# Attention in front of two feed-forward layers: transposes by row halves, a new order in a step, and another way for the softmax's inverse

## Chip, cores and metric

The kernel runs on one core of a Trainium2 chip. The metric is the device time of one execution in microseconds; lower is better. TensorE is PE in the profile (its weight loads PEld), VectorE is DVE, ScalarE is ACT, GpSimd is POOL and SyncE, which issues nearly all DMAs here, is SP.

## What is computed

```python
scores = scale * (q @ k.T)                    # B 2, H 8, S 576, D 64
x = psi_rel / psi_i                           # log1p of |i-j| over log1p of max(i,1)
bias = relu(x * w1 + b1) @ w2                 # 32 hidden units, one value per head
attn = exp(s - max(s)); attn /= sum(attn) + 1e-9     # s = scores + bias
x = (attn @ v) as (1152, 512)
x = prelu(x @ w_in, alpha) @ w_out            # 512 -> 2048 -> 512
out = (P(h) / Q(h)) @ w_out2, h = x @ w_in2   # rational activation
```

All inputs and the output are fp32.

## The kernel before

The attention is cut into nine blocks of 128 query rows (`BLOCKS`, four row blocks of each batch and one that holds the last 64 rows of both), and each block into four steps of two heads: 36 steps, numbered 0 to 35. `scores` (L313) makes a step's two 128x576 score planes in four banks of PSUM, the two heads on the two halves of the array's rows. `row_max` (L333, DVE) adds the bias, writes the sum to SBUF and keeps the row's extreme in `nm`. `expo` (L345, ACT) takes the exponential and its row sum. `flip` (L353) transposes the step's 128x1152 plane on PE, nine blocks of 128x128: four of each head into a bank of `ps_t` (two buffers of one bank), and the ninth, which spans both heads, into a spare place beside the next step's scores. `flip_out` copies the blocks to SBUF: two copies of 128x512 on ACT (in a few steps, by the table `ON`, one of them on DVE) and one of 128x128 on DVE. `values` (L379) multiplies them with V two steps after the scores. So in the place of step n, PE runs the scores of n, the transposes of n-1 and the values of n-2.

The bias is made beside that. Each of 36 `row`s takes four `hidden` operations (L222, 128x576, on DVE or ACT), eight matmuls in two halves (`bias_mm`, L235), an eviction for each half (`bias_out`, L249, DVE or ACT) and a DMA into the bias tile (`bias_move`, L267, on SP's queue). The eight rows of the first tile come before step 0, the other 28 within steps up to step 27.

When a block's fourth step is done, `inverse` (L398, DVE) makes the eight inverse row sums of each query. Blocks 0 to 5 turn them by a matmul with the identity (`inverse_flip`, L405), copy that out, store it to DRAM and read it back spread over partitions (`inverse_spread`, L412); blocks 6 to 8 spread it by eight matmuls (`inverse_on_tensor`, L429). `block_out`, `block_scale` and `block_split` (L421 to L451) take the block from PSUM, multiply it and split it into a high and a low part for the next layer; the low part is GpSimd's only work in the attention.

The order of all this is a list of due times (class `Agenda`): every piece is put on it with a time worked out from the tables' numbers (`Z`), the list is sorted, and each engine gets its instructions in that order. The numbers set an order, not a duration. From step 28 on, the bias is done and the first five weight units of the feed-forward layers (`unit_one`, `unit_two`, L654 on) come between the steps, on ACT and DVE. After step 35 the two feed-forward layers take PE to the end.

```python
ag.at(next_t + Z[f"new_flip{u}"] if new else t + DT + Z["flip0"] + Z["flip1"] * u, flip, n, u)
ag.at(t + DT + Z["fout0"] + Z["fout1"] * u, flip_out, n, u)
```

## Time and profile before

| what | us |
|---|---|
| three timed runs | 600.17, 601.75, 601.97 |
| median | 601.75 |
| span of the profiled execution, first to last instruction | 600.0 |
| time around the span, by the three runs | 0.2 to 2.0 |
| PE busy in the span | 584.8 (97%) |
| DVE, ACT, POOL busy | 496.7, 433.1, 23.7 |
| scores of step 0, 3, 28, 35 start at | 20.90, 37.79, 153.77, 184.99 |

The profiled execution's own time is not listed apart from its span; the table's fourth line says what can lie around it. A busy time is a union of spans, so an engine with overlapping instructions is not counted twice. A row of a timeline merges neighbours of one kind and gives their start, the time from the first start to the last end, and their count. A fp32 matmul leaves two records, a transpose one. Starts that follow each other give the time that a piece takes on PE, since ends overlap the next piece.

### The profile page before, as it was taken

The page shows a single profiled execution, that of the slowest core. Times are in us where ns is not written, and L with a number is a line of the kernel's source. Part 1 is how long each engine was busy: PE and PEld are TensorE (multiplying, and loading weights), DVE is VectorE, ACT ScalarE, POOL GpSimd, SP SyncE. Part 2 cuts the span into 40 slices and gives each one's busy share as a digit, 9 for nine tenths or more (in the row PEclk, how much of TensorE's full clock was granted, in tenths as well). Part 3 has the DMA queues.
Part 4 walks back from the last instruction along what each step waited for, and adds up shares of the span by engine and source line. Part 5 has one row for each costly group of instructions (what it writes and reads, how often), then busy time and mean ns, then how long its engine had stood idle before and what let it go on. Part 6 is the DMA issues. An engine that isn't in the chain of part 4 may idle for free.

```text
span 600.0 us, 11975 instructions
## 1 busy us (share of the span) xinstructions
PE 584.8 (97%) x4798; PEld 504.4 (84%) x4798; DVE 496.7 (83%) x837; ACT 433.1 (72%) x728; POOL 23.7 (4%) x23
## 2 busy tenths in 40 slices
PE   8899999999988999999999999999999999999997
PEld 4366666676757999999999999998999999899985
DVE  6688787877798767689998779989999999779784
ACT  6678989889777666676675567787777887655660
POOL 0000000000000000000000302000000000000000
PEclk9899999999999999999999999999999999999999
DMA  5894333342632334445555376867000000001011
GB/s 167 256 239 117 86 85 91 88 118 64 165 103 76 108 104 141 138 143 148 173 162 162 129 210 215 230 200 262 9 1 1 0 1 1 2 1 52 1 52 52
DMA packets 41238, 65.31 MB, mean 109 GB/s; under 512 B 4016, under 2 KB 23776, under 8 KB 41184
## 3 DMA queue, kind: packets, MB, share of 16 engines
q1 hardware_dynamic: 41040, 64.21, 36.5%
q8 instruction: 37, 0.61, 0.4%
q10 hardware_dynamic: 144, 0.35, 0.2%
q14 instruction: 17, 0.14, 0.1%
HBM read 47.35 MB, written 6.58 MB: 90 GB/s over the span
## 4 chain that ended last, share of the span: by engine, by line
PE 84%; DVE 8%; ACT 3%; DMA 2%; issue 2%; SPq 0%; DVEq 0%; ACTq 0%
PE ops L695 30%; PE hps L680 30%; PE bps L244 7%; PE s L326 6%; PE pv L389 5%; PE tp L365 4%; DVE p L338 1%; DVE mid L623 1%; PE s L361 1%; DVE w L649 1%; DMA away<-mid 1%; DVE mid L626 1%; DMA bias<-be 1%; DMA sm<-in_small_dram 1%; ACT p L349 1%
## 5 line engine op out<-in xcount | busy, mean ns | idle before, releaser
L680 PE MATMUL hps<-xh,w 128*128 128x384 f32 x768 | 204.1, 336 | 0.5 <-DVE nm L338 0.5
L680 PEld LDWEIGHTS hps<-xh,w 128*128 128x128 f32 x768 | 139.6, 188 | 1.9 <-DVE nm L338 0.7
L680 PE MATMUL hps<-xl,w 128*128 128x384 f32 x384 | 128.7, 335 | 0.0
L695 PE MATMUL ops<-g,w 128*128 128x384 f32 x576 | 104.5, 336 | 0.0
L695 PE MATMUL ops<-w,g 128*128 128x512 f32 x432 | 102.5, 392 | 1.2 <-DVE acc L767 1.2
L695 PEld LDWEIGHTS ops<-g,w 128*128 128x128 f32 x576 | 100.8, 188 | 0.0
L695 PEld LDWEIGHTS ops<-w,g 128*128 128x128 f32 x432 | 80.7, 188 | 17.6 <-issue 1.5
L349 ACT ACTIVATE p<-p,nm 128x576 f32<-128x576 f32 x72 | 55.6, 773 | 24.2 <-DVE nm L338 24.0
L680 PEld LDWEIGHTS hps<-xl,w 128*128 128x128 f32 x384 | 72.1, 188 | 0.9
L750 ACT CAST g<-n 128x768 fp32r<-128x768 f32 x48 | 40.0, 834 | 38.3 <-DVE n L714 26.5
L338 DVE CUSTOM_DVE_ANT_0 p<-s,bias 128x576 f32<-128x576 f32 x72 | 52.2, 755 | 17.6 <-PE s L326 8.7
L623 DVE SCALAR_TENSOR_TENSOR mid<-mid,raw 128x512 int32<-128x512 int32 x64 | 47.8, 747 | 13.5 <-ACT mid L615 13.3
L244 PE MATMUL bps<-h,w2s 128*32 128x288 f32 x576 | 51.2, 420 | 4.1 <-DVE be L258 2.5
L230 DVE TENSOR_SCALAR h<-tt,sc,nb 128x576 f32<-128x576 f32 x98 | 52.3, 573 | 0.0
L755 DVE TENSOR_TENSOR g<-n,g 128x768 fp32r<-128x768 f32 x48 | 46.5, 969 | 6.6 <-ACT g L750 6.6
L626 DVE SCALAR_TENSOR_TENSOR mid<-raw,mid 128x512 int32<-128x512 int32 x64 | 47.4, 740 | 2.2
L389 PEld LDWEIGHTS pv<-pt,v 128*32 128x32 f32 (+1 forms) x1320 | 40.8, 116 | 7.7 <-issue 1.8
L645 ACT CAST w<-mid 128x512 fp32r<-128x512 f32 x64 | 39.2, 614 | 10.8 <-PE hps L680 10.6
L389 PE MATMUL pv<-pt,v 128*32 128x128 f32 (+2 forms) x1320 | 46.6, 267 | 0.0
L619 ACT ACTIVATE raw<-raw 128x512 int32<-128x512 uint32 x64 | 43.4, 678 | 4.3 <-DMA raw<-in_moe_w_out_dram 2.6
L326 PE MATMUL s<-kt,q 64*128 64x288 f32 (+1 forms) x320 | 45.9, 433 | 0.0
L649 DVE TENSOR_TENSOR w<-mid,w 128x512 fp32r<-128x512 f32 x64 | 44.6, 699 | 0.0
(73 smaller groups left out, 723.4 us busy)
## 6 DMA issues: line engine op xcount, KB each, us to landing
raw<-in_moe_w_in_dram SPq DMA_DIRECT2D x32, 512.0 KB, 4.5
raw<-in_moe_w_out_dram SPq DMA_DIRECT2D x32, 512.0 KB, 3.7
bias<-be SPq DMA_DIRECT2D x32, 288.0 KB, 3.9
away<-mid SPq DMA_DIRECT2D x16, 256.0 KB, 4.8
mid<-away SPq DMA_DIRECT2D x16, 256.0 KB, 4.7
v<-in_vp_dram SPq DMA_DIRECT2D x10, 256.0 KB, 5.3
kt<-in_kT_dram SPq DMA_DIRECT2D x8, 288.0 KB, 5.8
out_dram<-acc SPq DMA_DIRECT2D x9, 256.0 KB, 2.1
```

What stands on the lines that cost most here:

```text
L230: nc.vector.tensor_scalar(out=h, in0=x, scalar1=sc[:, k : k + 1], scalar2=nb1, op0=ALU.mult, op1=ALU.max)
L244: nc.tensor.matmul(out=ps[32 * c : 32 * c + 32], lhsT=w2s, rhs=hid[j, r, c][:, u * HALF : (u + 1) * HALF], start=True, stop=True,)
L326: nc.tensor.matmul(out=pps[n, u][cols, w, :HALF], lhsT=queries[k][rows, hp, cols], rhs=KT[bb][rows, hp, w * HALF : (w + 1) * HALF], start= ...
L338: nc.vector.tensor_tensor_reduce(out=ptile[n][:, u, :].rearrange("p (w j) -> p w j", w=2), in0=pps.pop((n, u))[:, :, :HALF], in1=bias[j][: ...
L349: nc.scalar.activation(out=p, in_=p, func=AF.Exp, bias=nms.pop((n, u)), scale=-1.0, accum_out=sums[k][:, h : h + 1])
L389: nc.tensor.matmul(out=pv[64 * u + d : 64 * u + d + wide, hp, cols], lhsT=V[bb][:, j, 2 * hp + u, d : d + wide], rhs=pt[:, 4 * u + j if j ...
L623: nc.vector.scalar_tensor_tensor(out=m, in0=m, scalar=3, in1=raw[:, :, 0], op0=ALU.logical_shift_left, op1=ALU.bitwise_or)
L626: nc.vector.scalar_tensor_tensor(out=m, in0=raw[:, :, 1], scalar=-(2 ** 31), in1=m, op0=ALU.bitwise_and, op1=ALU.bitwise_or)
L649: nc.vector.tensor_tensor(out=w[:, 1, :], in0=mids.pop(j), in1=w[:, 0, :].bitcast(F32), op=ALU.subtract)
L680: nc.tensor.matmul(out=ps, lhsT=a, rhs=b, start=(i == 0), stop=(i == len(prs) - 1))
L695: nc.tensor.matmul(out=ops[ly, c, m], lhsT=a, rhs=b, start=(f == fs[0] and i == 0), stop=(f == fs[-1] and i == 2))
L755: nc.vector.tensor_tensor(out=gt[:, 1], in0=tmp.pop(p), in1=gt[:, 0].bitcast(F32), op=ALU.subtract)
```

## The change

`flip` now takes each block of 128x128 as two halves of 64 rows: each is a transpose of 64x128 with a 64x64 identity, and the two halves go to two banks and use the two halves of the array's rows, as the scores do. `ps_t` becomes one buffer of two banks, and the scores' tile one buffer of four banks (`s4`), in which the ninth block's halves lie. `flip_out` copies all eight blocks with one ACT instruction of 128x1024 (in steps 32 and 34 one half each on ACT and DVE). The order is written from labels of a step: the ninth block first, then the eight, one bias row for each of the steps 1 to 26, and from step 27 on other labels. Two rows of the second bias tile (`at_once`) move ahead of step 0. The inverse of blocks 0 to 7 is turned by one DVE transpose in 32x32 blocks, stored as 128 rows of 128 bytes (`inverse_store`) and read back spread; only block 8 is spread by matmuls. GpSimd's branches (`split_pool`, `again_pool`) are not in `ON`, so those copies stay where they were. The tables of numbers are new throughout; two lines of `ON` stand for them here.

```diff
@@ ON, Z (tables)
-    "first_hidden_scalar_2", "first_hidden_scalar_6", "flip_vector_28", "flip_vector_32",
+    "first_bias_scalar_6", "first_bias_scalar_7", "first_bias_scalar_8", "first_hidden_scalar_2",
...
@@ pools and first constants
-    ps_t = open_pool("ps_t", 2, "left", PSUM)
+    ps_t = open_pool("ps_t", 1, "left", PSUM)
     ps_b = open_pool("ps_b", 1, "left", PSUM)
-    ps_s = open_pool("ps_s", 2, "right", PSUM)
+    open_pool("ps_f", 2, "right", PSUM)
+
+    def scores_psum():
+        close_pool("ps_f")
+        open_pool("ps_s", 1, "right", PSUM)
...
+    inv = ac.tile([P, 2, 32], F32, name="inv")
+    nc.vector.memset(inv[:, 0], 0.0)
...
@@ bias rows
+    def at_once(j, r):
+        return j == 0 or j == 1 and r < 2
+
     def bias_mm(j, r, u):
-        if j > 0:
+        if not at_once(j, r):
             ps = ps_b.tile([P, HALF], F32, tag="b", name="bps")
             bps[j, r, u] = ps
         else:
             if u == 0:
-                bps[j, r] = ps_s.tile([P, 2, 512], F32, tag="s", name="bps2")
+                pool = pools["ps_f" if j == 0 else "ps_t"][1]
+                bps[j, r] = pool.tile([P, 2, 512], F32, tag="f" if j == 0 else "t", name="bps2")
             ps = bps[j, r][:, u, :HALF]
...
@@ scores
+        s4 = pools["ps_s"][1].tile([P, 2, 2, 512], F32, tag="s", name="s")
         for u in range(2):
-            pps[n, u] = ps_s.tile([P, 2, 512], F32, tag="s", name="s")
+            pps[n, u] = s4[:, u]
...
-        spare[n] = pps[n, 1][:, 1, HALF : HALF + P]
+        spare[n] = s4[:, :, 1, HALF : HALF + 64]
...
@@ flip, flip_out
-    def flip(n, u):
-        p = ptile[n]
-        if u == 0:
+    def flip(n, cols):
+
+        p = ptile[n].rearrange("p u j -> p (u j)")
+        if cols == 8:
             ptt[n] = pt_p.tile([P, 9, P], F32, tag="pt", name="pt")
-
-        beside = u == 2 and FIRST <= n + 1 < LAST
-        tp = spare[n + 1] if beside else ps_t.tile([P, 512], F32, tag="t", name="tp")
-        if u == 2:
-            nc.tensor.transpose(out=tp[:, :P], in_=p.rearrange("p u j -> p (u j)")[:, 512:640], identity=ident)
-        else:
-            for j in range(4):
-                o = 64 * u + j * P
-                nc.tensor.transpose(out=tp[:, j * P : (j + 1) * P], in_=p[:, u, o : o + P], identity=ident)
-        tps[n, u] = tp
-
-    def flip_out(n, u):
-        tp, pt = tps.pop((n, u)), ptt[n]
-        if u == 2:
-            nc.vector.tensor_copy(out=pt[:, 8, :], in_=tp[:, :P])
-        else:
-            out = pt[:, 4 * u : 4 * u + 4, :].rearrange("p j i -> p (j i)")
-            if u == 1 and f"flip_vector_{n}" in ON:
-                nc.vector.tensor_copy(out=out, in_=tp)
-            else:
-                nc.scalar.copy(out=out, in_=tp)
+            if n + 1 == NSTEP:
+                tps[n, 8] = ps_b.tile([P, HALF], F32, tag="b", name="tp8")[:, :P]
+                nc.tensor.transpose(out=tps[n, 8], in_=p[:, 512 : 512 + P], identity=ident)
+                return
+            out, blocks = spare[n + 1], [(0, 512)]
+        else:
+            out = ps_t.tile([P, 2, 512], F32, tag="t", name="tp")
+            blocks = [(64 * j, j * P if j < 4 else j * P + P) for j in range(8)]
+        tps[n, cols] = out
+        for o, a in blocks:
+            for w in range(2):
+                half = slice(64 * w, 64 * w + 64)
+                nc.tensor.transpose(out=out[:, w, o : o + 64], in_=p[half, a : a + P], identity=ident[half, half])
+
+    def flip_out(n, cols):
+        tp, pt = tps.pop((n, cols)), ptt[n]
+        if cols == 8:
+            out = pt[:, 8] if n + 1 == NSTEP else pt[:, 8].rearrange("p (w i) -> p w i", w=2)
+            nc.vector.tensor_copy(out=out, in_=tp)
+            return
+        out = pt[:, :8].rearrange("p j (w i) -> p w j i", w=2)
+        tp = tp.rearrange("p w (j i) -> p w j i", i=64)
+        if f"flip_vector_{n}" in ON:
+            nc.scalar.copy(out=out[:, 0], in_=tp[:, 0])
+            nc.vector.tensor_copy(out=out[:, 1], in_=tp[:, 1])
+        else:
+            nc.scalar.copy(out=out, in_=tp)
...
-        wide = 32 if FIRST <= n + 2 < 28 else D
+        wide = 32 if n + 2 < 27 else D
...
@@ inverse
     def inverse(k):
-        rs = sm_p.tile([P, H], F32, tag="rs", name="rs")
-        nc.vector.tensor_scalar_add(rs, sums.pop(k), 1e-9)
-        nc.vector.reciprocal(out=rs, in_=rs)
-        nc.vector.tensor_scalar_mul(rs, rs, WUP ** -3)
+        rs = inv[:, 0, :H].rearrange("p (u c) -> p c u", u=2)
+        nc.vector.tensor_scalar_add(rs, sums.pop(k).rearrange("p (c u) -> p c u", u=2), 1e-9)
+        nc.vector.reciprocal(out=inv[:, 0, :H], in_=inv[:, 0, :H])
+        nc.vector.tensor_scalar_mul(inv[:, 0, :H], inv[:, 0, :H], WUP ** -3)
         rts[k] = rs
-
-    def inverse_flip(k):
-        tp = ps_t.tile([P, 512], F32, tag="t", name="tp")
-        nc.tensor.transpose(out=tp[:H, :P], in_=rts[k], identity=ident)
-        rt = xu_p.tile([H, P], F32, tag="rt", name="rt")
-        nc.vector.tensor_copy(out=rt, in_=tp[:H, :P])
-        rts[k] = rt
+        if not by_tensor(k):
+            nc.vector.transpose(out=inv[:, 1], in_=inv[:, 0])
+
+    def inverse_store(k):
+        rd = dr_p.tile([4, 32, 32], F32, tag="rd", name="rd")
+        nc.sync.dma_start(out=rd.rearrange("q f i -> (q f) i"), in_=inv[:, 1])
+        rts[k] = rd
 
     def inverse_spread(k):
-        rd = dr_p.tile([H, P], F32, tag="rd", name="rd")
-        nc.sync.dma_start(out=rd, in_=rts.pop(k))
-        rb = xu_p.tile([P, 4, P], F32, tag="rb", name="rb")
+        rb, rd = xu_p.tile([P, 4, 4, 32], F32, tag="rb", name="rb"), rts.pop(k)
         for u in range(2):
-            src = rd.rearrange("(c u) i -> u c i", u=2)[u : u + 1]
-            nc.sync.dma_start(out=rb[64 * u : 64 * u + 64], in_=src.to_broadcast([64, 4, P]))
-        xus[k] = rb
+            src = rd[:, 4 * u : 4 * u + 4].rearrange("q c i -> q (c i)").unsqueeze(0)
+            nc.sync.dma_start(
+                out=rb[64 * u : 64 * u + 64].rearrange("p q c i -> p q (c i)"), in_=src.to_broadcast([64, 4, P])
+            )
+        xus[k] = rb.rearrange("p q c i -> p c q i")
...
     def by_tensor(k):
-        return k >= 6
+        return k == 8
...
@@ block_split
-        nc.scalar.copy(out=xh, in_=xu)
+        if k < 8 and "split_pool" in ON:
+            nc.gpsimd.tensor_copy(out=xh, in_=xu)
+        else:
+            nc.scalar.copy(out=xh, in_=xu)
...
@@ the agenda
     def step_time(n):
+        return T0 + DT * min(n, NB_) + DTL * max(n - NB_, 0)
+
+    for r in range(8):
+        at0 = Z["row0"] + (r - 1) * Z["row_step"]
+        bias_rows(0, r, Z["row0"] + r * Z["row_step"], Z["row_step"], at0, Z["row_step"])
+    ag.at(T0 - 0.05, scores_psum)
+    STEP_OF = {(j, r): 8 * j - 9 + r for j in range(1, 5) for r in range(n_rows(j))}
+    for (j, r), n in STEP_OF.items():
+        if at_once(j, r):
+            t = T0 + Z["pre"] + Z["pre_step"] * r
+            if r == 0:
+                ag.at(0.1, bias_tile, j)
+            for c in range(4):
+                ag.at(t + Z[f"pre_hid{c}"], hidden, j, r, c)
+            for u in range(2):
+                ag.at(t + Z["pre_mm"] + 0.1 * u, bias_mm, j, r, u)
+                ag.at(t + Z["pre_out"] + 0.1 * u, bias_out, j, r, u)
+            ag.at(t + Z["pre_out"] + 0.3, bias_move, j, r)
...
@@ a step
+        ag.at(label("flip", n + 1), flip, n, 8)
+        ag.at(label("flip", n + 1) + 0.05, flip, n, 0)
+        ag.at(label("fout8", n + 1), flip_out, n, 8)
+        ag.at(label("fout", n + 1), flip_out, n, 0)
+        ag.at(label("values", n + 2), values, n)
...
```

A step on PE, before, in steps 3 to 26 (`s` scores, `tp` and the first `s<-ident,p` transposes, `bps` bias, `pv` values; the last row comes in every fourth step):

```order
L326 MATMUL s<-kt_132,q 128x288 x4
L361 MATMUL s<-ident,p 128x128
L365 MATMUL tp<-ident,p 128x128 x8
L244 MATMUL bps<-h,w2s 32x288 x4
L389 MATMUL pv<-pt,v_133 32x128 x20
L244 MATMUL bps<-h,w2s 32x288 x4
L407 MATMUL tp<-ident,rs 8x128
```

and with the change:

```order
L325 MATMUL s<-kt_134,q 128x288 x4
L369 MATMUL s<-ident,p 128x64 x2
L369 MATMUL tp<-ident,p 128x64 x16
L261 MATMUL bps<-h,w2s 32x288 x4
L395 MATMUL pv<-pt,v_135 32x128 x20
L261 MATMUL bps<-h,w2s 32x288 x4
```

The places of the pieces are the same; nine transposes became eighteen of half the width, and the transpose of the inverse is gone from PE.

ACT in a step, before (`p` exponentials, `pt` the copy of the transposes, `h` a hidden row, `be` a bias eviction, `xu` a block's copy):

```order
L349 ACTIVATE p,sums<-p,nm 128x576
L228 ACTIVATE h<-tt,sm,sc 128x576
L377 COPY pt<-tp 128x512
L423 COPY xu<-pv 128x512
L349 ACTIVATE p,sums<-p,nm 128x576
L377 COPY pt<-tp 128x512
L256 ACTIVATE be<-bps,cv 128x288
```

and with the change:

```order
L383 COPY pt<-tp 128x2x8x64
L348 ACTIVATE p,sums<-p,nm 128x576 x2
L273 ACTIVATE be<-bps,cv 128x288
L461 CAST xh_892<-xu 128x4x128
L241 ACTIVATE h<-tt,sm,sc 128x576
```

One copy of four dimensions takes the place of two, it stands ahead of both exponentials of the step, and the eviction and the hidden rows follow them.

PE at the first steps, before, from the half bias row ahead of step 0's scores (`wps` are matmuls that only keep PE busy):

```order
L244 MATMUL bps<-h,w2s 32x288 x4
L326 MATMUL s<-kt_131,q 128x288 x4
L186 MATMUL wps<-ident 128x128 x2
L244 MATMUL bps<-h,w2s 32x288 x8
L326 MATMUL s<-kt_131,q 128x288 x4
L244 MATMUL bps<-h,w2s 32x288 x4
L365 MATMUL tp<-ident,p 128x128 x4
L244 MATMUL bps<-h,w2s 32x288 x4
L365 MATMUL tp<-ident,p 128x128 x4
L361 MATMUL tp<-ident,p 128x128
```

and with the change, from the first of the two bias rows that moved ahead:

```order
L261 MATMUL bps_332<-h,w2s 32x288 x8
L199 MATMUL wps<-ident 128x128 x2
L261 MATMUL bps_360<-h,w2s 32x288 x8
L325 MATMUL s<-kt_133,q 128x288 x4
L199 MATMUL wps<-ident 128x128 x2
L325 MATMUL s<-kt_133,q 128x288 x4
L369 MATMUL s<-ident,p 128x64 x2
L369 MATMUL tp<-ident,p 128x64 x16
L261 MATMUL bps<-h,w2s 32x288 x8
L325 MATMUL s<-kt_133,q 128x288 x4
```

The bias rows that stood between the scores of steps 0 and 1 now stand ahead of step 0, and step 1's scores follow step 0's at once.

## Rows read from the trace of the kernel before

**Rows 1.** Busy time by stretch: window, length, busy us per engine (instructions), granted clock, DMA.
```profile
0.00:37.79 37.79, 32.44 (x318) 17.53 (x318) 26.23 (x61) 25.47 (x42) 0.70 (x6) 0.95 0.80 224
37.79:153.77 115.98, 115.76 (x1819) 77.71 (x1815) 92.39 (x246) 101.34 (x216) 6.41 (x5) 1.00 0.38 100
153.77:184.99 31.22, 27.36 (x340) 20.62 (x336) 24.61 (x58) 26.16 (x57) 2.56 (x2) 1.00 0.48 137
...
200.00:300.00 100.00, 100.00 (x585) 99.58 (x585) 79.50 (x123) 66.94 (x114) 1.29 (x1) 1.00 0.46 138
```

**Rows 2.** Timeline of PE, one step: start, us, engine, line, operation, tiles, shape, count.
```profile
51.74 1.24 PE L326 MATMUL s<-kt,q 64*128 64x288 f32 x8
52.91 0.33 PE L361 MATMUL s<-ident,p 128*128 128x128 f32 x1
53.08 1.04 PE L365 MATMUL tp<-ident,p 128*128 128x128 f32 x8
54.05 0.69 PE L244 MATMUL bps<-h,w2s 128*32 128x288 f32 x8
...
56.34 0.51 PE L326 MATMUL s<-kt,q 64*128 64x288 f32 x2
```

**Rows 3.** Timeline of PE's weight loads in the same step, the transposes.
```profile
52.91 0.14 PEld L361 LDWEIGHTS s<-ident,p 128*128 128x128 f32 x1 [0.38 <-ACT p L349]
52.97 0.91 PEld L365 LDWEIGHTS tp<-ident,p 128*128 128x128 f32 x8
```

**Rows 4.** Weight loads of that step's scores, two short windows.
```profile
51.74 0.19 PEld L326 LDWEIGHTS s<-kt,q 64*128 64x128 f32 x2 [0.47 <-DVE h L230]
...
51.85 0.19 PEld L326 LDWEIGHTS s<-kt,q 64*128 64x128 f32 x2
```

**Rows 5.** That step's last two pairs of scores on PE, two short windows.
```profile
52.33 0.41 PE L326 MATMUL s<-kt,q 64*128 64x288 f32 x2
...
52.58 0.41 PE L326 MATMUL s<-kt,q 64*128 64x288 f32 x2
```

**Rows 6.** Timeline of PE after step 35: the values matmuls of the last block.
```profile
190.08 1.39 PE L389 MATMUL pv<-pt,v 128*64 128x64 f32 x40
```

**Rows 7.** Timeline of ACT in a step: a copy of transposes and what follows it.
```profile
87.57 0.57 ACT L377 COPY pt<-tp 128x512 f32<-128x512 f32 x1
88.04 0.50 ACT L256 ACTIVATE be<-bps,cv 128x288 f32<-128x288 f32 x1
```

**Rows 8.** The page's groups: copies on ACT.
```profile
L750 ACT CAST g<-n 128x768 fp32r<-128x768 f32 x48 | 40.0, 834 | 38.3 <-DVE n L714 26.5
...
L645 ACT CAST w<-mid 128x512 fp32r<-128x512 f32 x64 | 39.2, 614 | 10.8 <-PE hps L680 10.6
```

**Rows 9.** Timeline of DVE: the first and the last operation of an inverse.
```profile
82.74 0.16 DVE L400 TENSOR_SCALAR rs<-sums 128x8 f32<-128x8 f32 x1
...
83.18 0.17 DVE L402 TENSOR_SCALAR rs<-rs 128x8 f32<-128x8 f32 x1
```

**Rows 10.** Timeline of PE, the first steps.
```profile
25.94 1.19 PE L244 MATMUL bps<-h,w2s 128*32 128x288 f32 x8 [2.54 <-DVE be L258]
27.06 2.17 PE L326 MATMUL s<-kt,q 64*128 64x288 f32 x8
...
37.79 1.24 PE L326 MATMUL s<-kt,q 64*128 64x288 f32 x8
```

**Rows 11.** Timeline of DVE: the second row maximum of step 0.
```profile
24.70 0.75 DVE L338 CUSTOM_DVE_ANT_0 p<-s,bias 128x576 f32<-128x576 f32 x1
```

**Rows 12.** Busy time by stretch, columns as in the first group.
```profile
26.00:28.00 2.00, 2.00 (x12) 0.95 (x14) 0.86 (x2) 1.98 (x5) 0.00 (x0) 0.50 1.04 363
```

**Rows 13.** Timeline of PE: an inverse on PE and two steps of the tail.
```profile
164.45 1.09 PE L434 MATMUL tp<-ident,rs 128*64 128x128 f32 x16
...
176.45 0.33 PE L361 MATMUL s<-ident,p 128*128 128x128 f32 x1 [2.21 <-ACT p L349]
...
181.67 0.33 PE L361 MATMUL s<-ident,p 128*128 128x128 f32 x1 [1.64 <-ACT p L349]
```

More of the change, by code (lines that the diff above doesn't have):

```diff
@@ L252, in bias_out @@
         out, add = bev[j, r], cv[:, int(on_scalar(j, r, 2)) : int(on_scalar(j, r, 2)) + 1]
-        if j > 0:
+        if not at_once(j, r):
             half, ps = out[:, u * HALF : (u + 1) * HALF], bps.pop((j, r, u))
@@ L276, in bias_again @@
     def bias_again(h):
-        nc.vector.tensor_copy(out=bias[4][64:, h : h + 2], in_=bias[4][:64, h : h + 2])
-    def bias_rows_beside(j, r, at, step, at0, step0):
-        z, z0 = step / 4.1, step0 / 4.1
-        for c in range(4):
-            ag.at(at0 + z0 * Z[f"hidden{c}"], hidden, j, r, c)
-        for u in range(2):
-            x = at + Z[f"bias_mm{u}"] * z
-            n = max((n for n in range(FIRST, LAST) if step_time(n) <= x), default=None)
-            if n is None:
-                ag.at(x, bias_mm, j, r, u)
-                t = at + Z[f"bias_out{u}"] * z
-            else:
-                t = max(x, step_time(n) + Z["beside"])
-                ag.at(t, bias_mm, j, r, u)
-                key = "scalar" if f"bias_scalar_{j}{u}" in ON else "vector"
-                t = max(step_time(n) + Z[f"bo_{key}{int(t - step_time(n) >= Z['values'])}"], t + 0.1)
-            ag.at(t, bias_out, j, r, u)
-        ag.at(max(at + Z["bias_move"] * z, t + 0.1), bias_move, j, r)
+        eng = nc.gpsimd if "again_pool" in ON else nc.vector
+        eng.tensor_copy(out=bias[4][64:, h : h + 2], in_=bias[4][:64, h : h + 2])
     def bias_rows(j, r, at, step, at0, step0):
@@ L434, in inverse_on_tensor @@
             nc.tensor.matmul(
[L435 removed]
+                out=tp[64 * u : 64 * u + 64, c], lhsT=rts[k][:, c, u : u + 1].to_broadcast([P, 64]), rhs=ident,
                 start=True, stop=True,
@@ L441, in block_scale @@
         xu, rb = xus[k]
+        if not by_tensor(k):
+            xu = xu.rearrange("p c (q i) -> p c q i", q=4)
         nc.vector.tensor_tensor(out=xu, in0=xu, in1=rb, op=ALU.mult)
@@ L470, in step_time, with label @@
     def step_time(n):
[L471 to L487 removed]
+        return T0 + DT * min(n, NB_) + DTL * max(n - NB_, 0)
[15 more added lines that the diff above has]
+            ag.at(t + Z["pre_out"] + 0.3, bias_move, j, r)
+            continue
+        t = step_time(n)
+        h = t - DT
+        if r == 0:
+            ag.at(t + Z["bias_o1"] + 0.15, bias_tile, j)
+        for c in range(4):
+            ag.at(h + Z[f"hid{c}"], hidden, j, r, c)
+        for u in range(2):
+            ag.at(t + Z[f"bias_b{u}"], bias_mm, j, r, u)
+            ag.at(t + Z[f"bias_o{u}"], bias_out, j, r, u)
+        ag.at(t + Z["bias_o1"] + 0.2, bias_move, j, r)
+    EARLY = step_time(STEP_OF[4, 3]) + Z["bias_o1"] + 0.3
+    def label(key, n):
+        return step_time(n) + Z[key + ("_tail" if n >= NB_ else "")]
     for n in range(NSTEP):
```

91 lines of the change are left out of this document (35 added, 56 removed), and 24 rows, old and new, of the table Z.

## Prediction

> **What bounds the kernel now.** I read three views in this order: busy time by stretch, the timeline of each engine in one step, and the weight loads beside it.
>
> The stretches [rows 1] cut the span at the scores of steps 3, 28 and 35. From step 3 to 28, 115.98 us, PE is busy 115.76, ACT 101.34 and DVE 92.39: PE bounds the 25 steps, at 4.64 us each, and ACT is next at 4.05. From step 28 to 35, 31.22 us, PE has 27.36 and ACT 26.16: neither fills it. From 200 us on PE is full (100.00 of 100), so what attention saves before that arrives at the end whole, and what ACT or DVE save there arrives not at all.
>
> One step on PE [rows 2], by starts: the scores 1.17, the first transpose 0.17, the other eight 0.97, the rest 2.29, together 4.60. Eight transposes take 1.04 with 0.27 for the last one, so each follows the one before after 0.11. Its stream has 128 columns.
>
> The weight loads of the transposes [rows 3] say what else stands in those 0.11: the second load starts 0.06 after the first, when PE comes from other work and no stream holds it back; only then do eight loads take 0.91, one in 0.11. So the load of 128 columns of a transpose needs no more than 0.06, and the stream sets the 0.11. In the scores [rows 4] two loads of 64 rows start together (count 2, 0.19 in all), and the next two 0.11 later: the halves of the rows load side by side, but a load of an ordinary fp32 matmul is slower than that of a transpose.
>
> **The change, part by part.**
>
> *Row halves on PE.* Nine transposes become nine pairs. A pair streams 64 columns. The nearest stream of that width is in the values of the last block [rows 6]: 40 records on two halves of the columns, 20 pairs in 1.39, under 0.07 a pair, and 0.06 if the last one's end is some 0.2 as elsewhere. The load needs 0.06 too if it stays as it is at full height. I take 0.06, since both rows that bear on it say so. The ends are 0.05 (half of 0.11) and 0.22 (two halves one behind the other). At 0.06 the step loses 9 x 0.05 = 0.45.
>
> *No change of the array's division between scores and transposes.* Before, the last two pairs of scores start at 52.33 and 52.58 [rows 5], 0.25 apart, yet the first transpose follows only after 0.33, and the second follows the first after 0.17 instead of 0.11 [rows 2]: together about 0.15 a step, which should go, as the halves use the rows as the scores do. No row shows the two behind each other, so the bounds are 0 and 0.15; I take 0.15. PE's step is then 4.60 - 0.45 - 0.15 = 4.0.
>
> *The copies on ACT.* Two of 512 columns become one of 1024. Now one takes 0.47 from start to start [rows 7], two 0.94. From 512 to 768 columns a cast grows from 614 to 834 ns [rows 8], 0.86 ns a column, so 512 more columns add 0.44: about 0.91. ACT gains 0.03 a step, nothing that counts; if the copy's four dimensions cost extra, up to 0.2. The split between ACT and DVE stays about even, and no work goes to GpSimd. ACT's 4.05 a step is therefore the new bound, just above PE's 4.0.
>
> *The inverse.* PE loses a transpose of 8 columns in six of the 25 steps, no dearer than the first of a step (0.33, [rows 2]), and in the tail one of the two spreads by matmuls of 1.09 [rows 13] before step 35 for block 6 and one for block 7. DVE loses a small copy and gains a transpose of 128x32: between 0.17, an operation on 128x8, and 0.75, a row maximum [rows 9, 11]; I take 0.2, as it is nearer to the first. The inverse now stands ahead of the next step's row maxima, so in every fourth step these wait for the last exponential and for four operations, 0.6 for three of them [rows 9] and 0.2: that delays ACT's exponentials by 0 to 0.8, and I expect the copy, which now precedes them on ACT, to cover it. The store of 128 short rows and the two reads have more than a step before the scaling needs them; for blocks 6 and 7 they are six DMAs more on SP's queue. Behind each store a bias move waits, which has two steps of slack: nothing.
>
> *Steps 3 to 28.* PE needs 24 x 4.0 + 3 = 99, ACT 101, DVE 92. Engines so close cannot all be full; I add 4 for waits on each other and take 105.5. Gain 10.5 (5 to 14).
>
> *The front.* The first row maxima wait for the bias and end at 25.45 [rows 11]. Before, PE stood still 2.54 until 25.94, made a half bias row first and started step 1's scores at 27.06 [rows 10], which took 2.17 as the granted clock was 0.50 there, the 1.2 GHz level [rows 12]. Step 3 starts 10.7 after that [rows 10], with five half rows and an idle stretch in between. With the two rows moved ahead, step 1 can start near 25.5, step 2 when DVE has made three hidden rows, two maxima, one eviction and one copy, some 3.7 later, and step 3 one step after that: 33.5 against 37.79. The halved clock may still meet it, and the moved rows may hold step 0 back. I take 3.5 (0 to 5).
>
> *The tail.* PE stood still 2.21 and 1.64 for exponentials [rows 13]. Its 27.36 shrink by 7 x 0.6 and two spreads to about 21; ACT's 26.16 hardly change. So ACT sets it: 26.5 for 31.22, gain 4.7 (1 to 6). Step 35 on: the same pieces, nothing.
>
> **Sum.** 10.5 + 3.5 + 4.7 = 18.7. The profiled span of 600.0 becomes 581.3. The median of the runs, 601.75, lies 1.75 above that span; I carry the same distance, 583.0.
>
> **A rule against it.** The rows on which the 0.06 rests are those of the transposes at full height; the scores' rows show 0.11 for 128 columns at half height. If a half transpose loads as a score does, a pair takes 0.11, and halving the stream wins nothing; that is the first rival below. The Trainium skill, "TensorE: Matmul & The Clock Gate", section "LDWEIGHTS (loading the stationary operand)", has it so: a load's time goes by its columns at 1.2 GHz and not by its rows, by which 128 columns are estimated at 107 ns. The trace agrees in the scores (0.11) and not in the transposes (0.06).
>
> **The rivals.**
>
> 1. *A pair takes 0.11.* For it: the loads of the scores [rows 4], the only ones at half height. Against it: the 0.06 between the first two loads of a transpose [rows 3]. PE's step is 4.45, 24 x 4.45 + 3.4 = 110.2, with 0.9 for waits 111, gain 5; the tail, on ACT, keeps 4.4, the front 3.2: 601.75 - 12.6 = 589.
>
> 2. *The steps stay at 4.6, held by ACT.* One copy for both heads, one buffer of two banks, and the exponentials behind the copy: flips, copy, exponentials and next flips form one ring. For it: ACT already waits for DVE and PE in each step, and 4.05 of work leaves little room. Against it: the copy and the exponentials take about 2.5, and the remaining 1.5 of ACT's work lies where PE makes the next transposes. Then 24 x 4.6 + 3.5 = 114, gain 2, with 5.5 of front and tail: 594, to 598 if the tail stays too.
>
> 3. *Slower: the halves go one behind the other.* If transposes of 64 rows don't run side by side, a pair takes 0.22, PE's step 4.45 + 9 x 0.11 = 5.4, and the 25 steps 24 x 5.4 + 4.4 = 134, 18 more than now; the tail gains nothing, the front 2. 601.75 + 18 - 2 = 618. It decides from about 0.155 a pair, where the steady steps lose what front and tail give. Against it: the scores do run so [rows 4]. For it: no row shows a transpose on part of the rows.
>
> **How the numbers follow.** Runs of this kernel lie 0.3% apart, so a change under 0.3% can't be told from none. Forecast 0.60, first rival 0.17, second 0.11, third 0.09; 0.03 for mishaps that eat the gain. The forecast alone runs from 576 (front 5, waits of 1) to 588. In it lies the case that the 0.15 between scores and transposes stays: PE's step 4.15, 24 x 4.15 + 3 = 103 with the same 4 for waits, 585. The range 575 to 597 takes in the first two rivals and leaves out the third. Faster 0.88, same 0.03, slower 0.09.
>
> **What would show it.** In the profile after: the eighteen transposes of a step within about 0.6 and the weight loads in pairs 0.06 apart (0.11: rival 1; each half alone: rival 3); no gap between scores and transposes; scores of neighbouring steps about 4.2 apart, ACT busy over 95% between steps 3 and 28 (PE waiting for `p` with ACT full is the forecast, PE waiting with ACT idle is rival 2); step 3 near 34, step 28 near 140, step 35 near 166; PE full from 200 us on as before. A start of step 3 later than 37, or idle PE in the feed-forward layers, would make the prediction wrong in a way that I have not priced.

## The result, and the profile after

The changed kernel takes 575.1 us (median; 573.6 to 576.9), the kernel before in the same session 601.9: a ratio of 0.956, with an interval of 0.9538 to 0.9582. The forecast was 583.0, the range 575 to 597. The sign is right, but the gain is 26.8 where 18.7 was forecast, the median lies in the range by 0.1 us, two of the four runs (573.6, 574.7) lie below it, and the band of 576 to 588 that the prediction gave to its own mechanism is missed. The profiled execution is the fastest of the four runs; its span is 571.9 us, 28.1 less than that of before. By the stretches of the prediction, in spans:

| stretch | before | after | gain | forecast |
|---|---|---|---|---|
| to step 3's scores | 37.79 | 33.54 | 4.25 | 3.5 |
| step 3 to 28 | 115.98 | 99.89 | 16.1 | 10.5 |
| step 28 to 35 | 31.22 | 26.20 | 5.0 | 4.7 |
| step 35 to the end | 415.0 | 412.3 | 2.75 | 0 |

Busy time by stretch, after (columns as in [rows 1]):

```profile
0.00:33.54 33.54, 28.90 (x336) 16.63 (x336) 24.66 (x60) 26.61 (x41) 0.70 (x6) 1.00 0.77 224
33.54:133.43 99.89, 99.34 (x2018) 72.75 (x2015) 90.48 (x247) 97.74 (x190) 7.85 (x6) 1.00 0.51 127
133.43:159.63 26.20, 22.90 (x367) 17.39 (x367) 22.67 (x58) 24.34 (x49) 1.27 (x1) 1.00 0.55 156
```

In the 25 steps PE and ACT are now both full to within 0.6 and 2.2 us. In the tail ACT is the fullest, as forecast.

One step on PE and its weight loads, after:

```profile
94.17 1.24 PE L325 MATMUL s<-kt,q 64*128 64x288 f32 x8
95.24 0.22 PE L369 MATMUL s<-ident,p 64*128 64x64 f32 x2
95.30 0.67 PE L369 MATMUL tp<-ident,p 64*128 64x64 f32 x16
95.89 0.69 PE L261 MATMUL bps<-h,w2s 128*32 128x288 f32 x8
...
98.16 1.24 PE L325 MATMUL s<-kt,q 64*128 64x288 f32 x8
```

```profile
95.00 0.14 PEld L369 LDWEIGHTS s<-ident,p 64*128 64x128 f32 x2
95.24 0.58 PEld L369 LDWEIGHTS tp<-ident,p 64*128 64x128 f32 x16
```

The first pair starts 1.07 after the scores (1.17 before, [rows 2]) and the next 0.06 later (0.17 before). Sixteen loads take 0.58 with 0.14 for the last: eight pairs, 0.06 apart. The first two loads start while the last scores still stream. From the scores to the bias row it is 1.72, where it was 2.31.

ACT in the steps, after, from copy to copy:

```profile
79.99 1.02 ACT L383 COPY pt<-tp 128x1024 f32<-128x1024 f32 x1
...
92.13 1.01 ACT L383 COPY pt<-tp 128x1024 f32<-128x1024 f32 x1
93.04 0.78 ACT L348 ACTIVATE p<-p,nm 128x576 f32<-128x576 f32 x1
...
96.19 1.01 ACT L383 COPY pt<-tp 128x1024 f32<-128x1024 f32 x1
```

The copy takes 0.91 to the next start, and four steps take 16.20, 4.05 each, with no gap on ACT; the next four take 16.09. The groups of ACT in these 25 steps (shape and count, busy us, mean ns, idle before them):

```profile
L348 ACT ACTIVATE p<-p,nm 128x576 f32<-128x576 f32 x50 | 38.7, 784 | 0.6 <-DVE nm L337 0.6
L383 ACT COPY pt<-tp 128x1024 f32<-128x1024 f32 x24 | 24.3, 1014 | 1.1 <-PE tp L369 1.0
```

Before, the same group of exponentials had 14.6 us of idle time in front of it, for row maxima.

Steps of PE range from 3.92 to 4.41, apart from step 6 (4.62, a wait for V) and step 27 (3.08, without a bias row). The 4.41 stands once, in step 15; on PE and on DVE it is:

```profile
81.90 1.24 PE L325 MATMUL s<-kt,q 64*128 64x288 f32 x8
...
85.68 0.69 PE L261 MATMUL bps<-h,w2s 128*32 128x288 f32 x8
86.31 1.24 PE L325 MATMUL s<-kt,q 64*128 64x288 f32 x8
```

```profile
82.17 0.69 DVE L450 TENSOR_TENSOR xu<-xu,rb 128x512 f32<-128x512 f32 x1 [0.27 <-issue]
82.78 1.07 DVE L243 TENSOR_SCALAR h<-tt,sc,nb 128x576 f32<-128x576 f32 x2
83.76 0.75 DVE L337 CUSTOM_DVE_ANT_0 p<-s,bias 128x576 f32<-128x576 f32 x1
...
85.12 0.51 DVE L275 TENSOR_SCALAR be<-bps,cv 128x288 f32<-128x288 f32 x1
```

In one step of four VectorE multiplies a block by its inverse. The row maximum then starts 1.86 after the scores (1.33 to 1.45 in the steps beside it), the eviction ends at 85.63, and the second half bias row, which needs the one buffer that it empties, starts at 85.68: PE waits some 0.45, which the modelled ends of the values hide in its busy time. In the same step of the next blocks (11, 19, 23) the step takes 4.05 or 4.06. Of all steps of 3.99 and more, but for steps 4, 6 and 20, the second half bias row starts 0.05 or 0.06 after VectorE's eviction ends; in the steps of 3.92 to 3.94 it follows by 0.09 to 0.13. By the starts, the 25 steps cost PE 97.2 of its own work (24 x 3.92 + 3.08) and 2.7 beyond it, 0.7 of them in step 6.

### The profile page after: what moved, and what is told of

Read it like the earlier page. It is cut to its first block, busy times and chain, and to the rows that moved or that the text cites. A ratio compares the mean times of both kernels' runs of the same rounds, so it can differ in the third digit from the quotient of the medians.

```text
span 571.9 us, 12499 instructions
## 1 busy us (share of the span) xinstructions
PE 559.1 (98%) x5063; PEld 494.8 (87%) x5063; DVE 489.0 (86%) x835; ACT 432.5 (76%) x697; POOL 23.5 (4%) x23
## 4 chain that ended last, share of the span: by engine, by line
PE 88%; DVE 4%; DMA 3%; ACT 3%; issue 1%; SPq 0%; ACTq 0%
PE hps L703 35%; PE ops L718 35%; PE bps L261 6%; PE pv L395 5%; PE s L325 5%; DMA v<-in_vp_dram 2%; PE tp L369 2%; DVE p L337 1%; ACT h L241 1%; DMA rd<-inv 1%; ACT p L348 1%; DMA sm<-in_small_dram 1%; ACT be L280 0%; DVE mid L646 0%; DVE mid L649 0%
## 5 line engine op out<-in xcount | busy, mean ns | idle before, releaser
L773 ACT CAST g<-n 128x768 fp32r<-128x768 f32 x48 | 40.0, 834 | 28.1 <-DVE n L737 19.6
L646 DVE SCALAR_TENSOR_TENSOR mid<-mid,raw 128x512 int32<-128x512 int32 x64 | 46.4, 726 | 8.0 <-ACT mid L638 7.8
L243 DVE TENSOR_SCALAR h<-tt,sc,nb 128x576 f32<-128x576 f32 x98 | 51.0, 573 | 0.5 <-PE bps L261 0.4
L395 PE MATMUL pv<-pt,v 128*32 128x128 f32 (+2 forms) x1300 | 47.8, 267 | 0.8 <-DMA v<-in_vp_dram 0.8
L649 DVE SCALAR_TENSOR_TENSOR mid<-raw,mid 128x512 int32<-128x512 int32 x64 | 45.7, 714 | 2.2
L325 PE MATMUL s<-kt,q 64*128 64x288 f32 (+1 forms) x320 | 44.5, 425 | 2.3 <-issue 1.9
```

Source lines behind the costliest of these rows:

```text
L243: nc.vector.tensor_scalar(out=h, in0=x, scalar1=sc[:, k : k + 1], scalar2=nb1, op0=ALU.mult, op1=ALU.max)
L325: nc.tensor.matmul(out=pps[n, u][cols, w, :HALF], lhsT=queries[k][rows, hp, cols], rhs=KT[bb][rows, hp, w * HALF : (w + 1) * HALF], start= ...
L395: nc.tensor.matmul(out=pv[64 * u + d : 64 * u + d + wide, hp, cols], lhsT=V[bb][:, j, 2 * hp + u, d : d + wide], rhs=pt[:, 4 * u + j if j ...
L646: nc.vector.scalar_tensor_tensor(out=m, in0=m, scalar=3, in1=raw[:, :, 0], op0=ALU.logical_shift_left, op1=ALU.bitwise_or)
L649: nc.vector.scalar_tensor_tensor(out=m, in0=raw[:, :, 1], scalar=-(2 ** 31), in1=m, op0=ALU.bitwise_and, op1=ALU.bitwise_or)
```

## The experiments

The changed kernel's own runs spread over 3 us. One cause is V: in the profiles of the variants that leave it where it is, PE waits up to 2.8 us for it at step 6 (not at all in the two runs with full-height transposes). Small differences are therefore read from the scores of step 12 to those of step 28, 16 steps behind that place. The variants that leave these steps alone (rows back, inverses on PE, V earlier, weight units set back) take 63.31 to 63.55 there; the run without warming took 64.69, with one wait of 1.30 ahead of step 28.

| kernel | step 12 to 28, us | ratio to before (interval) |
|---|---|---|
| changed | 70.00 to 133.43: 63.43 | 0.956 (0.9538 to 0.9582) |
| full height | 74.68 to 145.76: 71.08 | 0.9757 (0.974 to 0.9773) |
| ninth at full height | 73.07 to 140.49: 67.42 | 0.9647 (0.9632 to 0.9661) |
| two copies | 71.29 to 135.54: 64.25 | 0.9575 (0.9558 to 0.9592) |
| GpSimd's copies | 75.01 to 138.51: 63.50 | 0.9561 (0.9522 to 0.96) |
| V earlier | 70.45 to 133.76: 63.31 | 0.9557 (0.9536 to 0.9579) |
| multiplication later | 72.77 to 140.38: 67.61 | 0.9653 (0.9629 to 0.9677) |
| hidden row to ACT | 72.12 to 136.47: 64.35 | 0.9588 (0.9569 to 0.9607) |
| hidden row to GpSimd | 70.37 to 132.79: 62.42 | 0.9548 (0.9528 to 0.9568) |

### All transposes at full height

```diff
...
-        for o, a in blocks:
-            for w in range(2):
-                half = slice(64 * w, 64 * w + 64)
-                nc.tensor.transpose(out=out[:, w, o : o + 64], in_=p[half, a : a + P], identity=ident[half, half])
+        for j, (o, a) in enumerate(blocks):
+            c = j % 4 * P
+            nc.tensor.transpose(out=out[:, j // 4, c : c + P], in_=p[:, a : a + P], identity=ident)
...
```

> The changed kernel with all nine transposes at full height again (128x128, eight of them into the two banks, the ninth into one spare place); one copy, the order and all else as changed. Theory (the row halves carry the gain of the steps): each transpose costs 0.11 instead of 0.06 and the drain between scores and transposes comes back with 0.15, so PE's step grows by 0.6 to about 4.6, 32 steps lose 15 to 19 us: 590 to 594, with PE full in steps 3 to 28 and 4 us of idle ACT there more. Rival (the new order and the single copy carry it, the halves are beside the point): 575 to 578.

Measured: 587.45. PE, one step:

```profile
97.19 1.24 PE L325 MATMUL s<-kt,q 64*128 64x288 f32 x8
98.36 0.33 PE L362 MATMUL s<-ident,p 128*128 128x128 f32 x1
98.53 1.04 PE L370 MATMUL tp<-ident,p 128*128 128x128 f32 x8
...
101.69 1.24 PE L325 MATMUL s<-kt,q 64*128 64x288 f32 x8
```

Every step with a bias row takes 4.50 with PE full (111.60 of 111.60), and ACT idles 10.3 us ahead of its copies. The cause is the halves: the step's own cost on PE falls by 0.58 (4.50 to 3.92), against 0.60 worked out. The time falls by 12.4 and not by 15 to 19: the changed kernel's steps are 4.0 and not 3.92, as ACT and VectorE keep the rest, and the tail, where PE has waits, takes 26.87 and not 26.20, only 0.67 for seven steps.

The halves carry 12.4 of the 26.8. The rest is still there at full height: by the spans of this run and of before 14.8, of which 3.6 lie up to step 3, 4.4 in steps 3 to 28, 4.4 in the tail and 2.4 behind step 35. Which of the other parts of the change brings how much of it is only in part separated below.

### The ninth block alone at full height

```diff
...
+            tps[n, 8] = spare[n + 1]
+            nc.tensor.transpose(out=spare[n + 1], in_=p[:, 512 : 512 + P], identity=ident)
+            return
...
```

> The changed kernel with the ninth block alone at full height, between the scores and the eight blocks in halves: one transpose of 128x128 for one pair, and two changes of the array's division more in a step. Theory (such a change costs PE a drain, 0.15 to 0.3 for both): a step grows by 0.2 to 0.35, the time by 6 to 12 us, and the first transpose starts about 0.33 after the last pair of scores and not 0.24. Rival (a change of division costs nothing, only the wider stream counts, 0.05 a step): 1 to 2 us more, 576 to 577.

Measured: 580.9, and every step from 5 to 26 takes 4.27 or 4.28:

```profile
98.71 1.24 PE L325 MATMUL s<-kt,q 64*128 64x288 f32 x8
99.88 0.33 PE L362 MATMUL s<-ident,p 128*128 128x128 f32 x1
100.14 0.71 PE L371 MATMUL tp<-ident,p 64*128 64x64 f32 x16
```

The first transpose follows the scores after 1.17 again, and the first half after another 0.26, where a pair follows after 0.06. The step is 0.35 longer (4.27 for 3.92). The wider stream is 0.05 of it, so the two changes of the array's division cost 0.30; that is in line with the 0.15 that the prediction took for one. In time it is 5.8, just under what was expected, for the reason just given.

### The copy in two

```diff
-            nc.scalar.copy(out=out, in_=tp)
+            for w in range(2):
+                nc.scalar.copy(out=out[:, w], in_=tp[:, w])
```

> The changed kernel with flip_out's copy as two ACT instructions of 128x512, one for each half of the rows, in place of one of 128x1024. Theory (ACT stands level with PE in steps 3 to 28, so that its work counts): 0.03 to 0.1 us a step more on ACT, 1 to 3 us more in all. Rival A (PE alone sets the steps): within 0.5 us of the changed kernel. Rival B (the copy's four dimensions cost extra, and two smaller ones are no dearer): 0 to 2 us less.

Measured: 576.5, which the runs can't tell from 575.1; 16 steps take 0.82 more, 0.05 a step, inside the theory. ACT is busy 0.98 more there: its work counts. The copy's four dimensions cost nothing that shows: one copy takes the 0.91 that was worked out.

### GpSimd makes the high part

The edit adds `"split_pool"` to `ON`.

> The changed kernel with its branch switched on in which GpSimd, and not ACT, makes the high part of blocks 0 to 7 (eight copies of 128x512, some 0.5 us each off ACT, one in every fourth step). Theory (PE and ACT are both full, PE a little more): the time stays within 1 us of the changed kernel while ACT's busy time in steps 3 to 28 falls by about 3 us. Rival A (ACT sets the steps, as the prediction had it): 2 to 4 us less. Rival B (the slower copies on GpSimd come late for the next block's work or hold VectorE up): 1 to 5 us more.

Measured: 575.4, between 573.5 and 578.9; 16 steps 63.50 against 63.43. ACT is busy 60.49 of them and not 62.22, and nothing is gained: of four steps, three take 3.92 to 4.0, and the fourth 4.34 or 4.35 each time, where the changed kernel has 4.05 (and once 4.41). VectorE is late there, and its two hidden operations, beside GpSimd's copy, take longer than the 1.07 shown above:

```profile
103.57 1.36 DVE L244 TENSOR_SCALAR h<-tt,sc,nb 128x576 f32<-128x576 f32 x2
```

```profile
103.72 0.89 POOL L460 CAST xh<-xu 128x512 fp32r<-128x512 f32 x1 [13.84 <-DVE xu L451]
```

So rival B has part in it: what ACT is spared, some 0.5 in four steps, VectorE loses by 0.29. What relief of ACT alone would give, this run doesn't show.

### The two bias rows back in their steps, and without warming matmuls

```diff
-        return j == 0 or j == 1 and r < 2
+        return j == 0
```

> The changed kernel with the two bias rows that moved ahead of step 0 back in steps of their own, as all other rows of their tile. Theory (the front's gain of 4.25 us up to step 3 comes from them): step 3's scores start 1.5 to 4 us later than 33.54, the span grows by as much: 576.5 to 579. Rival (the front's gain comes from the smaller steps and from a PE at full clock there, and the two rows only move from one place to another): within 0.7 us of the changed kernel's 575.1, or up to 1 us less.

The second run also takes `"warm_11"` out of `ON`.

> The changed kernel with the two bias rows back in their steps, as in the run on them alone, and without the two matmuls that only keep PE busy between the scores of steps 0 and 1. PE then does nothing for about 2.1 us ahead of step 1's scores (before the change it was 2.54, after which the granted clock was 0.50 and those scores took 2.17 in place of 1.24). Theory (the front's gain comes in good part from PE not falling to the lower clock): the clock falls to 0.50 there, step 1's scores take 2.17, step 3 starts 1 to 2 us later than the 33.97 of the run on the rows alone. Rival (2.1 us are harmless): clock 1.00, step 3 at 34.0, the time that of the run on the rows alone, 576.1.

Measured: 576.1 and 575.65, neither to be told from 575.1. The scores of the first steps start at:

| kernel | step 0 | 1 | 2 | 3 |
|---|---|---|---|---|
| before | 20.90 | 27.06 | 31.83 | 37.79 |
| changed | 22.35 | 25.18 | 29.07 | 33.54 |
| rows back | 21.27 | 26.09 | 29.98 | 33.97 |
| rows back, no warming | 21.57 | 26.38 | 30.27 | 34.27 |
| full height | 22.57 | 25.40 | 29.66 | 34.16 |

PE in the run without warming:

```profile
25.76 0.69 PE L261 MATMUL bps<-h,w2s 128*32 128x288 f32 x8 [2.07 <-DVE be L275]
26.38 1.24 PE L325 MATMUL s<-kt,q 64*128 64x288 f32 x8
```

The theory falls in both. Without the two rows ahead, 3.8 of the front's 4.25 us remain, and without the halves 3.6. PE can stand 2.07 us here and still has a granted clock of 1.00, with scores of 1.24 and not 2.17. What remains lies, by the rows, in three places: the idle 2.54 of before [rows 10] is 1.43 with the rows back; the half bias row and the scores behind it ran at the lower clock, 1.19 and 2.17 for 0.69 and 1.24; and ahead of step 3 a third half row and a wait of 0.65 are gone. Before, and with the rows back:

```profile
37.17 0.69 PE L244 MATMUL bps<-h,w2s 128*32 128x288 f32 x8 [0.65 <-ACT be L256]
```

```profile
25.46 0.69 PE L261 MATMUL bps<-h,w2s 128*32 128x288 f32 x8 [1.43 <-DVE be L275]
```

Which number of the order brings each was not tried.

### The inverses of blocks 6 and 7 on PE again

```diff
-        return k == 8
+        return k >= 6
```

> The changed kernel with the inverses of blocks 6 and 7 spread by matmuls again, as before the change (two times 1.09 us on PE between steps 27 and 35; VectorE loses two transposes, SP's queue six DMAs). Theory (ACT, busy 24.34 of 26.20 us there, sets the tail, and PE stands in it 3.3 us): 0 to 1 us more. Rival (PE sets it): 2 us more, 577. Other side (the read back through DRAM is late there): up to 1 us less.

Measured: 588.2, 13 us more, which neither theory had. PE:

```profile
142.48 1.09 PE L440 MATMUL tp<-ident,inv 128*64 128x128 f32 x16 [0.45 <-ACT pt L383]
143.50 0.28 PE L369 MATMUL s<-ident,p 64*128 64x64 f32 x2
147.70 1.09 PE L369 MATMUL tp<-ident,p 64*128 64x64 f32 x16 [3.93 <-DVE xu L450]
148.73 2.40 PE L395 MATMUL pv<-pt,v 128*64 128x128 f32 x20
...
169.61 1.12 PE L369 MATMUL tp<-ident,p 64*128 64x64 f32 x16 [4.36 <-DVE xu L450]
```

The matmuls themselves take the 1.09 expected. But the spread lies in `ps_t`, now one buffer, until VectorE has multiplied the block by it, a step later, and the next eight transposes wait for that buffer: 3.93 and 4.36 us. PE then comes back at the lower clock (the mean granted is 0.66 from 147 to 152 us; the values take 2.40 for 1.31). So the new way of the inverse is not a small saving beside the halves: in this order, with VectorE's multiplication where it stands, the halves' one buffer of two banks needs it. An earlier multiplication was not tried.

### V earlier

```diff
-    "step_v1": 3.72,
+    "step_v1": 2.4,
```

> The changed kernel with the last part of batch 1's V issued one place earlier on SP's queue: ahead of the store of the first block's inverse, which waits 4 us for VectorE, and of its two reads back. Theory (the 0.49 us for which PE stands at step 6's values, and the 4.62 of that step, come from the place on the queue): that step takes 3.95, the time falls by 0.5 to 0.9 us, and the runs lie closer together, as the run with GpSimd's copies lost some 4 us at this place. Rival (the loads are late by themselves, whatever their place): within 0.3 us.

Measured: 575.3, no difference, though the wait is gone. In the changed kernel SP's queue and PE show:

```profile
43.51 1.66 SPq L422 DMA_DIRECT2D rb<-rd  x2
45.21 0.59 SPq L215 DMA_DIRECT2D v<-in_vp_dram  x1
```

```profile
49.34 0.42 PE L395 MATMUL pv<-pt,v 128*32 128x128 f32 x8 [0.49 <-DMA v<-in_vp_dram]
```

V's last part stands behind the inverse's two reads. Moved ahead, PE waits there no more: steps 3 to 28 take 99.25 for 99.89. But in this run step 3 starts 0.97 later: step 0 already starts 0.53 later, and two waits for batch 0's V, of 0.31 and 0.26, stand where the changed kernel has one of 0.34. The DMA engines are full there in both (share 1.05 and 1.06 from 24 to 36 us). So the place on the queue is the cause of that wait, and what it is worth is less than the runs can show.

### VectorE's multiplication later

```diff
-    "bscale": 3.6, "bsplit": 5.33,
+    "bscale": 6.6, "bsplit": 7.6,
```

> The changed kernel with VectorE's multiplication of a block by its inverse (0.69 us, one in four steps) behind the next step's row maxima and bias eviction in place of ahead of them; the split into two parts follows later too. Theory (in steps 3 to 28 the 3.92 us of PE's own work are held up in every fourth step, 4.41 or 4.34, since the second half bias row waits for VectorE's eviction of the first, which comes late behind this multiplication): six steps lose 0.3 to 0.45 us each, 1.8 to 2.7 us in all, about 573. Rival A (ACT, busy 3.91 us a step, holds the mean at 4.0 wherever VectorE's work stands): within 0.5 us. Rival B (the ninth block's copy, now behind the multiplication, makes the values late): 0.5 to 2 us more.

Measured: 580.6, a miss on the other side. The held step falls to 4.18, but the next rises to 5.00, and PE now waits openly:

```profile
94.08 0.69 PE L261 MATMUL bps<-h,w2s 128*32 128x288 f32 x8 [0.64 <-DVE be L275]
```

The row maxima of that step stand behind the four operations of the next inverse, as in the changed kernel, but one of the four takes 0.89 and not 0.17. First the changed kernel, then this run on DVE and on GpSimd, whose subtraction for the low part has moved beside the inverse:

```profile
87.19 0.17 DVE L408 TENSOR_SCALAR inv<-inv 128x8 f32<-128x8 f32 x1
```

```profile
90.98 0.89 DVE L408 TENSOR_SCALAR inv<-inv 128x8 f32<-128x8 f32 x1
```

```profile
90.54 1.30 POOL L462 TENSOR_TENSOR xl<-xu,xh 128x512 fp32r<-128x512 f32 x1 [15.63 <-ACT xh L461]
```

VectorE's operation ends 0.03 after GpSimd's, at 91.87, and so it is, within 0.04, in the three other blocks from 70 us on: 0.7 of the 1.1 us is this collision, which no theory had. So the place behind the row maxima is the worse of the two with the split where the edit put it; with the split elsewhere it was not tried.

### One hidden operation off VectorE: to ACT, then to GpSimd

Both runs have V earlier and GpSimd's copies. The first gives ACT a second one of the four hidden operations (`c` = 2) of rows 0 and 4 of a tile:

```diff
+        if c == 2 and r in (0, 4) and j > 0 and not at_once(j, r):
+            return True
```

> The changed kernel with three edits together: V of batch 1 issued earlier, as in the run on V alone; the high part of blocks 0 to 7 made by GpSimd, as in the run on GpSimd alone; and, in the place that this frees on ACT, one more hidden row of each fourth step (rows 0 and 4 of a tile) moved from VectorE to ACT. Theory (every fourth step is held 0.4 us by VectorE's late eviction, and VectorE gets there earlier by one hidden row of 0.49 us): the steps of 4.34 to 4.41 become 3.95 to 4.0, six times, and no step waits for V: 571.5 to 573. Rival A (ACT, PE and VectorE are so close that the gain is given back in the next step): within 0.7 us of 575.1. Rival B (GpSimd's copies slow VectorE's operations beside them): 1 to 4 us more.

Measured: 577.6, above the changed kernel's median; 16 steps 0.92 more. The held step falls to 4.02, and the next takes 4.43: the row maxima there wait for the inverse, and that for an exponential.

```profile
89.36 0.18 DVE L408 TENSOR_SCALAR inv<-sums 128x8 f32<-128x8 f32 x1 [0.61 <-ACT p L350]
```

```profile
82.44 1.03 ACT L385 COPY pt<-tp 128x1024 f32<-128x1024 f32 x1
...
98.75 1.01 ACT L385 COPY pt<-tp 128x1024 f32<-128x1024 f32 x1
```

ACT needs 16.31 for the four steps, without a gap: rival A by its mechanism. The size, 2.5 us more, is rival B's, but VectorE's hidden operations are not slowed in the steps looked at. The profile's span is 3.1 longer, of which 0.92 lie in the 16 steps and 1.70 before step 3, with waits for batch 0's V of 1.28 and 0.18. So such an operation went to GpSimd:

```diff
+            pool = c == 1 and r in (0, 4) and j > 0 and not at_once(j, r)
+            (nc.gpsimd if pool else nc.vector).tensor_scalar(
```

> As the run with three edits, but the hidden row that leaves VectorE in each fourth step is made by GpSimd and not by ACT, so that neither of the two engines level with PE gets work for it. Theory (with the steps at 4.05 ACT ran without a gap: 16.2 us from copy to copy over four steps; with V early, ACT relieved of 0.5 and VectorE of 0.49 in every four steps, PE's own 3.92 is the step): 25 steps take 98.0 to 98.8 and not 99.89, the time is 572.5 to 574. Rival A (GpSimd's hidden row is so slow that PE waits for it): several us more, with PE waiting for a hidden row in every fourth step. Rival B (VectorE's operations beside GpSimd's take longer, as a pair of hidden rows of 1.07 us took 1.36 beside GpSimd's copy): 575 to 578.

Measured: 574.1 (573.2 to 576.0).

```profile
90.13 1.24 PE L326 MATMUL s<-kt,q 64*128 64x288 f32 x8
...
94.06 1.24 PE L326 MATMUL s<-kt,q 64*128 64x288 f32 x8
...
98.06 1.24 PE L326 MATMUL s<-kt,q 64*128 64x288 f32 x8
```

```profile
94.22 2.78 POOL L244 TENSOR_SCALAR h<-tt,sc,nb 128x576 f32<-128x576 f32 x1 [9.01 <-PE bps L262]
```

Steps 12 to 26 now take 3.92 to 4.00 each, none is held, and 16 steps take 62.42, 1.0 less than in the changed kernel: with both engines relieved, and GpSimd's copy beside a hidden operation that takes no longer for it, PE's own work sets the step. VectorE relieved without ACT was not run. The 25 steps take 99.11, above the 98.0 to 98.8 expected, as steps 4 and 7 take 4.50 each. The median is 1.0 lower too, but the intervals overlap: this version is the fastest here, and not shown to beat the changed kernel.

### The order of the weight units set back

Eleven numbers of `Z` (`m0`, `m1`, `tb`, `ud`, `ud0`, `ud2`, `ud2x`, `ujoin`, `uload`, `urest`, `ulow`) take their values of before.

> The changed kernel with eleven of the numbers that order the weight units and the feed-forward layers set back to those of before; the attention up to step 27 is as changed. Theory (after step 35 the change saved 2.75 us, of which 1.24 were one wait of PE for VectorE's sum near 413 us and 0.47 one for a row maximum, and the new order of the weight units removed them): 1.0 to 2.0 us more, with a wait of PE for that sum in the layers. Rival (the shorter transposes of the last two steps and the free places in the queues carry it): within 0.5 us.

Measured: 587.4; from step 35 to the end 422.3 and not 412.3. PE's waits from 180 us on (line waited for, us in total, times, longest):

```profile
PE ops L718 <- DVE acc L790: 3.5, 1, 3.5
PE ops L718 <- DVE w L672: 1.5, 1, 1.5
```

The wait for VectorE's sum is back, and larger than before the change. Ten us, where one to two were expected: PE idles 6.0 us more there and is busy 4.0 more, at a mean granted clock of 0.99. This mixture of two orders is worse than either, so it doesn't tell what the new numbers brought over the old ones. That the numbers decide this stretch, with the attention's part of it unchanged, is shown; which of the eleven is not.

## Why the prediction was right, and where it was off

**A pair at 0.06, and no change of division: right.** Pairs come 0.06 apart, PE's step is 3.92 where nothing else holds it (4.0 forecast), and the two runs with full height give back 0.58 and 0.35. Rivals 1 and 3 are out. The rule behind rival 1, in the Trainium skill, "TensorE: Matmul & The Clock Gate", section "LDWEIGHTS (loading the stationary operand)", has a load go by its columns, by which 107 ns are estimated for 128; the trace of the changed kernel differs, with two such loads in each 0.06.

**The copy and ACT's 4.05: right.** 0.91 a copy, 16.20 for four steps. ACT has no gap of its own in the steps looked at, and 0.98 more of its work costs 0.82. Rival 2, a ring through the one buffer, is out: PE waits in the steady steps neither for `p` nor for `pt`. By the same rows the forecast's own sign, PE waiting for `p`, did not show: PE waits for VectorE's eviction.

**"Engines so close cannot all be full; I add 4 for waits": wrong, and so was the 101 below it.** This is the mis-sized term of the sum: 105.5 forecast, 99.89 measured, 5.6 of the 9.4 us by which the gain was too small. It has two parts. ACT idles 2.15 us in the stretch and not 4: the 14.6 us for which it waited before were no sign of waits to come, since ACT waited as PE was the bound, and when PE's work shrank so did they, to 0.6. The larger part is ACT's own work, busy 97.74 and not 101.34, 3.6 less. The run at full height has the changed kernel's ACT program, and there its busy time is 100.33 in 111.60 us, against 97.74 in 99.89: an instruction with idle time behind it counts to its own end, one that is followed at once only to the next start (a copy of 1.02 at 79.99 is followed after 0.89).

**The front: size right (4.25 for 3.5), cause wrong.** "With the two rows moved ahead" carries about 0.4 of it, so the size was luck.

**The tail: right** (26.20 for 26.5). That PE doesn't set it, the run at full height shows: 0.67 more, for 0.58 of work in each of seven steps. But the inverse was costed at PE's time alone, two times 1.09, and not at the buffer that it holds.

**"Step 35 on: the same pieces, nothing": wrong by 2.75.** The pieces are the same, but their order isn't, and PE was not without waits there before. Two rows of the trace of before that the prediction passed over:

```profile
187.80 0.44 PE L680 MATMUL hps<-xh,w 128*128 128x384 f32 x1 [0.47 <-DVE nm L338]
...
413.34 4.35 PE L695 MATMUL ops<-w,g 128*128 128x512 f32 x18 [1.24 <-DVE acc L767]
```

After the change PE has no wait past 180 us, but one of 0.47 for a copy just behind step 35's scores. Its idle time from there to the end falls from 5.72 to 4.31, 1.4 of the 2.75. The shorter transposes of the last two steps bring little of the rest: the run at full height takes 412.57 there, 0.3 more than the changed kernel. What brings the remaining 1.0 stays open. A stretch that reads 100.00 of 100 doesn't speak for the stretches beside it: from 325 to 425 us PE was at 98.76.

**The total: in the range by 0.1 us, which is luck.** The four stretches all gained more than forecast, so that no error made up for another.

## What to carry to other kernels

Where an engine waits because another is the bound, its waits go when the bound goes: don't carry them into the sum; take its work from start to start in a stretch without gaps, and then look for the one instruction of the third engine that comes late. An edit that shares or merges a buffer has to be costed with everyone who holds that buffer, and for how long: here a matmul of 1.09 us would have held the transposes for 4. When engines stand level, price what the relief of one costs the next: GpSimd's copy spared ACT some 0.5 in four steps and cost VectorE 0.29.
